# Causal attention values normalised on their way out of PSUM, by factors spread through DRAM

## The chip, the cores and the metric

One core of one Trainium2 chip runs the kernel; time is device microseconds of one execution, given as the median of several runs. The trace is of one profiled execution of the same program.

## The reference

Three stages over a batch of 4 with 448 tokens, in float32:

```python
# 1. twelve heads of 64: RMS-normalised q and k, softmax attention
q_n, k_n = rmsnorm(q, g_q), rmsnorm(k, g_k)
attn = softmax(q_n @ k_n^T / 8)            # denominators + 1e-9
x = heads_to_columns(attn @ v)             # [4, 448, 768]
# 2. mixer: tokens, then channels (768 -> 1536 -> 768)
u = x + transpose(relu(x^T @ w_tok1) @ w_tok2)
x = u + relu(u @ w_ch1) @ w_ch2
# 3. four experts, each one causal head of 64; every token keeps its best two
logits = x @ w_gate
for e in range(4):
    a = softmax(causal(x @ wq[e] @ (x @ wk[e])^T / 8))
    out += gate[:, e] * (a @ (x @ wv[e]) @ wo[e])
```

The gate of a token is the softmax over its best two logits, and 0 for the two other experts.

## The kernel before

All products are float32. The mixer and the projections split each operand into a high and a low part and run three passes on TensorE per product (`mm3`, line 625). Scores (line 707), attention values (line 830) and transposes (lines 731, 755 and 856) are float32 matmuls.

The batches go through the stages one after another. While batch b is in its channel mixer, the twelve heads of batch b + 1 run as six pairs in between (`pipeline`, `Pair`), and in front of them the two causal pairs of batch b - 1, whose expert projections (`project`) have just been made. Batch 2's causal pairs are scored between the channel mixer and the projections of batch 3, and batch 3's own come at the very end.

A pair's path is `score` (`weighted`: scores into PSUM, row maxima on VectorE, exponentials on ScalarE with row sums as a by-product; `flip` or `turn`: the weights transposed, so that keys lie on partitions) and `finish` (`attend`: the product with the values into a PSUM tile `av`, whose rows are 2 x 64 value columns and whose columns are the 448 queries). What remains is the division by the row sums, which lie on partitions, one per query, while `av` has queries along its columns. The kernel has two ways for that:

- The heads of batches 1 to 3 use `spread`: the inverse sums are turned into rows, written to DRAM, and read back broadcast over 64 partitions as a tile `rn`; `attend` then multiplies `av` by `rn` as it takes it out of PSUM (line 849). For pairs with queries in blocks of 112 (not `wide`) `spread` has a memset, an addition, a reciprocal, a 32-square transpose (`tni`), four DMA writes and two broadcast reads.
- The causal pairs, and the heads of batch 0, use `normalize`: `av` is copied to SBUF (`oT`), transposed by four matmuls per pair (line 856) so that queries lie on partitions, and multiplied by inverse sums (times the gate, for causal pairs) as it leaves PSUM into a tile `nat` (line 875). `combine` then transposes each half back by four matmuls, copies it out of PSUM and subtracts for the low part (line 1291), and multiplies with `wo` to make the output.

No instruction's place is left to a queue or to the compiler: every step is planned (`Plan.add` with an estimated cost, what it reads and writes, the engines that it may run on) and then issued in an order that stands in a constant, `TABLE`, with the engine of each step. The table was found by annealing, starting from a list scheduler (`lay`), which charges TensorE extra for a change of mode: `TURN` and `ENTRY`, for "rows" (scores), "columns" (values) and everything else. DMAs go through SyncE's queue, in order. VectorE and GpSimd share a port.

The tile `nat` has one buffer, which also holds the q and k rows of the next heads for their mean squares. PSUM tiles: `m` (values, transposes) has 2 buffers, `a` (products) 2, `s` (scores) 2.

Of the kernel before, what the change touches and what calls it, by code (L numbers as in the profile page):

```python
# [12 lines left out]
F32 = mybir.dt.float32  # L13
# [48 lines left out]
    r";`m5Bd2`j?+}<c+%~Mj&rCdmE3|=TH*f?d?$juYZ;$ZMdItlj+eAX-Qial?BK{3AURf|Y*>ZOM}A-l8{%R;G)W~)+=-KWrL4"
    r"LVI;@m=TZdM}GDoi%}lo=&eH|LBwU39=hih3C@7y&4U?SuurdO2q4Zohk2MOdIgYA<B@N_{JMT4B^6>0T+@f78jxKj@&^X?<"
    r"9A<zOdxg-hV;r`Q{f^A@ar5baHUeSc)MaBpjp;!nx=jP1}0sp_^XEp8`9ddwv`e>#%Zidgu$b=I;S6lk)e~T>kgdG4HjBt5#"
    r"3GZ%m)TudEw8`KIC<_MLeL6F@6kg1#^jD;LiR%w=Th0Q81<_1QdgWkzR$?c)h3x9?keKwYQKj)|-Kwc9LC(l^XQ3Ko_2-*y|"
    r"Yu>d`*Qn7hd(&x0#NGwdR%$W8%+dBNEkr`v2PsY0=P=RlxjNYHO5MO6<D`zh(&%k|cmjq(0IPYkAMk<TJMr9hvj$7>(U!*5h"
    r"=l^Xm27L_l-_OpWqyl}Ca1CBWpPfMaUHQ9Gg`l*`wwIp{{7~MJbvuBRqnB1Ep>^F^R2{mWN1z$oi$18s(Q>3$r1RBDStv`xw"
    r"%o(l@9I~^$ex}-mWW!Gj6FSYgx}ApO}dyAt;#6RIM1uTWBvJ*aP9Y*?Th=QmEtFUKiN(~@D#~v<dsy(-+Rz0;~+&@(wVG|XV"
    r"X{<ZU~PIxMM)+?q2P=M`am@Nwo71J=oXRBK1r)zfpqD2n8Lku%km0@!vuC<sj)?*D<Y<-`wA3L+-#BJNJLAr;OLG+)LTAlrc"
    r"Ex&@amh9UR>?1URw&>Is2wd7x?&1|T&FRROFYFH`m6%qLNB=F=J5t~t};Tq=q?xBTd})#>NUN_G!J2lg!R;8|&0PUVm9&Yuf"  # L70
    r"BhN`dszMHU*T8;nevtfY`o29P6j63J@SUt69XWtYy4G#nVNc!ijhug7xDO*~6L(t(>P&c@wMXLoT&>CC!ZC|+UU`ZZ3`uNfZ"
    r"$?A!#e&EuD288ZQS#+!;Cy);Ycm832tViLRZ9~7DyLA$;_@7C$O~W_;xH+%KW0RIIIfSH1m?`!oa;Ojfsu$|*5A&1mdFbN@E"
    r"}QQJYNj}kw0eNFpHp!vrNilLdOJAfy?)o)@R6igx9-@0R)diS%t5u-pIQ~cbfNy)KP6Nb4S%QNUXXeuG;+|AB07OS-F17;uL"
    r"&)G1tO?TxO>w?_H1Iah6zIkaS)OV$&<v^Kp(>1eHm|kyu9!Yhn8>cH}Sn|(64a-$Var{mff#oWYA%OGwZ}!8&LtaRd=oZg!I"
    r"LPd&=-qIriQDpBGVlJzhEhXB?;Je-|d;rH=;S<NbW;boR{jiPc!o7<Xm;6PXhWYZ0Qaj(hF#AirA&%p`@-uN6F4^D~?aXqfX"
    r"n!8y#plaC6{cmg@}lvr@z6U{MoIi?kelP_<58A-8a__Xido)3(9C%g&El5zE>>*rRa=U+E@`82}p0^~OP@Ro6}Va7e#e|Z6u"
    r"#;s{RbLUeXe|+S|6DwNG!1**ZPF;nD_dquWM+lkg$#Mk7B(ADhQaN=)3M7hOlH@WD!MrW7WA;NE`kgy~ql+IRNQfbW-Lxw7%"
    r"*t==HWmGVfsMs<4<}v3?DX)htAXpJUm|2*#hO(okVKM>=($$SXDy2S?T%EQlz?1Nft<)O<W%s(di>$ExY`g(3D28~$6ok30$"
    r"S1~!Xw2S9oCPS(eu)im;5|z`pXC}4v-y49){!2ANbv_0g;>J@{r0>P{=|8?q7-X;J5O7?zwJe5xARmbC=buxp&QN;JHE#e}_"
    r">uY**#OSQS}J5Ne1e=Dkgp?%26)PM=@P`|rkxf!Ul56Kdb-)wb67Q}F)$xouJQ_<bUY5#C~Jf_2%aA}erB=Wxd9Y<5p%`Kf#"  # L80
    r"GbjtmB3!?-)8Zi4xp59;EH{6CT>kGyvq&@K`A?x$KJVrO*?CRrKkr2A=IjP{aNIEHxvaGYUi8Xig^L6>lyZnrSJDt(ZQTM?x"
    r"irO``g`Y99ed($+##mnMGY_Fz6dzEhp(2|!e}CQ;KVdiDccnxof7gBu-pbBi?7yvl<dXr|%4mHKPI0#=V`mFX@5fD_Ef%9i9"
    r"X8&@-3uY|^A=}BazlO*KRfm-U$tk{k@kDq1TwR}2{-4bCnB+ap)(o}N!7bZ1FifhkERa%3%Yf#ywG3e^}BY532%6@XGe7e$@"
    r"#o&q{Pr)m!RMCq{D{Jhps(el3SBp6RG~1je3i8-`BG`v<(9)y5q;dIutZ?(Y5n3f8SjPa(FL4xNQ^Y?dxdE%(60Efjc?I))u"
    r"TAy8#%@Z>}Ya{)aBJ?pimN^ZEa-#%uy-!9kEtuv02*AZ0RP3+6n3;XuE+^sfiHRG<SrhDaq1T=(5Sj_p74Yuk3QH`hHelVX9"
    r"5oWtmtKbm(G;9_(BG5+7v@WM8JFaVS2zcJB{6(Emd%z`;9FolhK*=8g1wk+=WW2amD2O?8!(*EH_K^XW?|G<NTHNtHLGTvyH"
    r"Jj2;JfJtc20e;o3GLq4W=s;#p;E=a({*D}vA{-58I*gpCxovZpL$7uqej=y~ZXMRFZb;+tKE*xOrGAdf5Aq5M*NcCdgV*8!I"
    r"+9ap738TsY&Qg2X007s8&YvB%DROQGY4;ezh{fn$eR2F8utCMmb-TDLJxkuvO4LqbJEI|XVEA(1mt(H5eJ>4?Z`KG)NE_df!"
    r"QYX`ME!L2i6=%ATtToKSb8uk<9}w2o0y&@NGmg8~*i3_yA$yC9B^Z5Z*fEo>?s=<z<wI@nRP{kUJiWBVugf@=F-GoM7vq#Ku"
    r"rVh~sw4YqPsYI6W*MxrL)7vr?LsyqW&e9ymD|yA!fc<;rV25xNPHPXb47{JPusW$n;ga7gyLp4gQ^+40s-y&6OV7x2Ppv_AP"  # L90
    r"&kL)x2ZW~@JM@FHjaQ%pIy+lV)v2V2Y-d8Sha(4~?fSha*aVTz1K*Ig|=i^BG^onwNb>a_IY0k-k3RCqP3*^@Aq^~2KST|_v"
    r"Te#zj{Ud6>DZl<QzM$;QMmv^+)1zzm!l6NOE%x*hG=QUfw-n98ywI}l@8;t;w%i`OfrE(h(LO11Ce$2b?!DloaH_cSyEA7}q"
    r"pUhF#8WSnZmEyZIv!p=5B?Orio>@vJHXpo%S(7KNRI|<9Qx)gp@GNqF_PCT+U5J&z*X}Wi0SpwG<5sA8*U`RS-#>k=O`{OJc"
    r"Rn`4&`VbgS#Dki(uzNoqpt9=DCNKV%m#nk*w#+5?sd1;6{Ny&ZTxNDf1X|x8JyIvdxxXqlQIvQ_V5TKllAHxpm1E$Efq^fTQ"
    r"W?#2-{jME_N?Hja23!$U2~-yD^Q!vXx%W+$e=sWdH+s?P*0!6Rk7gaJ!jU>qcP0S_zwP2$ojgeE~)JckILpm1!KDI14K=dnv"
    r"UQgYzF!U$Kn0OS=$!!=Tq&2N-*yVEz^l6AI0%ra+ztV%Sz-Du|v9JH$B)fh^B+U7Kz$%n!uUR}Hu*UDy<eX1Tw3uo6Os}zCO"
    r"Cwbsoo#q<aoDe1as2IOqNjQQqw<j&(IN#HpYZeyE-ju=-^2=Y>A}Im+70s6N8SL&ihHS+UL8u>!RRxIfhoQpdd;)5@vW9oEk"
    r"-~DJJ7HJrw*TPpl9<Q#_a%)}9-_NDHSpB)avLj|zjoeZ^XG=^M_wt0MM`Fd!qXQb^oRoL>`-xcVaP0yLD#bcX9wv$OFW#=MX"
    r"1}+mq+%qkLX+9UQ>d)tA@WrhCelf&be<F_kS!-Jk~Xzl<pq6d4!Ek`Jvflu3f*f)C)F}E~=o{%Mhoki+OktdE{+kALS>L1O+"
    r"-M;+1`7vb}m5R@nAX*!+~p91-zX6%7Y%3M<fHSr+5}^q+h&eZ=&K_=dy87h~=U21nfzC;Ya$VPxp7d<}Eu8wLC;Tq~9`CigO"  # L100
# [1312 lines left out]
```

## Time and profile before

| | before |
|---|---|
| time of 3 runs | 839.68 us median, 838.71 to 841.11 |
| the profiled execution | 838.88 us, of which 837.1 us are the span of the trace |
| TensorE matmuls | 810.9 us busy, 97% of the span |
| VectorE, ScalarE, GpSimd | 614.6, 465.9 and 154.8 us |
| granted TensorE clock | 1.00 of full in every stretch but the last (0.97) |
| DMA | 168.37 MB |

An engine's busy time is the union of its instructions; a matmul's record lasts longer than its turn in the stream, since matmuls are pipelined, so the start of one to the start of the next is the better price of one.

### The profile page before, as it was taken

The numbers are of one execution on the slowest core, as the hardware profiler recorded it, in microseconds if no ns is written. First come the engines' busy times: TensorE is split into PE (matmuls) and PEld (weight loads), VectorE is DVE, ScalarE is ACT, GpSimd is POOL, SyncE is SP. The second block draws the span as 40 slices with busy tenths as digits, with TensorE's granted clock in tenths as the row PEclk, the third lists the DMA queues.
The fourth block names the chain that finished last, engine by engine and source line by source line (L and its number), as shares of the span: only waits on it lengthen the run. The fifth ranks groups of instructions, "written<-read, shape, count | busy, mean of one in ns | idle before, by whom it ended". The sixth has DMA issues, their size and how long they took to land.

```text
span 837.1 us, 13116 instructions
## 1 busy us (share of the span) xinstructions
PE 810.9 (97%) x4508; PEld 630.6 (75%) x4508; DVE 614.6 (73%) x1292; ACT 465.9 (56%) x1033; POOL 154.8 (18%) x181
## 2 busy tenths in 40 slices
PE   4899999999999999999999999999999999999998
PEld 1446697887676869877777877877876898999786
DVE  7999898889998785568889688756498773224473
ACT  6988976767887533644577446334576531000233
POOL 3043411122352244010230214000021010000000
PEclk9999999999999999999999999999999999999999
DMA  8747878988777748877566515785645416766444
GB/s 237 198 143 208 274 242 274 322 274 284 253 253 189 259 150 259 281 202 200 175 194 161 165 60 154 242 272 175 209 135 161 136 50 194 207 210 208 127 139 170
DMA packets 83201, 168.37 MB, mean 201 GB/s; under 512 B 17504, under 2 KB 39136, under 8 KB 83136
## 3 DMA queue, kind: packets, MB, share of 16 engines
q1 hardware_dynamic: 82992, 167.54, 65.7%
q8 instruction: 36, 0.59, 0.3%
q14 instruction: 29, 0.24, 0.1%
q10 hardware_dynamic: 144, 0.00, 0.0%
HBM read 136.66 MB, written 30.84 MB: 200 GB/s over the span
## 4 chain that ended last, share of the span: by engine, by line
PE 82%; DVE 12%; ACT 3%; issue 2%; DMA 1%; POOL 0%; SPq 0%; ACTq 0%; DVEq 0%
PE a L625 58%; PE s L707 9%; PE m L830 9%; PE m L856 2%; DVE nm L677 2%; DVE s L805 2%; PE s L755 2%; PE a L731 1%; DVE s L817 1%; ACT s L692 1%; PE s L731 1%; DVE wraw L575 1%; DVE wraw L577 1%; DMA h<-in_nat_dram 1%; DMA kept_c<-whl 0%
## 5 line engine op out<-in xcount | busy, mean ns | idle before, releaser
L625 PE MATMUL a<-uhl,whl 128*128 128x448 f32 x1152 | 242.9, 365 | 0.9 <-DVE hid L1203 0.9
L625 PEld LDWEIGHTS a<-uhl,whl 128*128 128x128 f32 x1152 | 213.3, 188 | 27.9 <-issue 8.7
L625 PE MATMUL a<-hid,whl 128*128 128x448 f32 x864 | 182.0, 365 | 0.8 <-DVE whl L555 0.7
L625 PEld LDWEIGHTS a<-hid,whl 128*128 128x128 f32 x864 | 160.0, 188 | 24.2 <-issue 6.4
L692 ACT ACTIVATE s<-s,nm,st 128x448 f32<-128x448 f32 (+1 forms) x192 | 137.3, 723 | 57.5 <-DVE nm L683 29.5
L817 ACT COPY s<-s 32x896 f32<-32x896 f32 (+1 forms) x118 | 102.5, 868 | 28.1 <-DVE s L805 18.4
L707 PE MATMUL s<-k,q 64*128 64x448 f32 (+4 forms) x512 | 110.1, 545 | 4.8 <-ACT s L692 3.9
L677 DVE TENSOR_REDUCE nm<-s 128x2 f32<-128x896 f32 (+1 forms) x96 | 101.6, 1080 | 13.0 <-PE s L707 12.5
L830 PE MATMUL m<-s,v 128*64 128x448 f32 x384 | 77.5, 545 | 0.9 <-POOL whl L555 0.9
L707 PEld LDWEIGHTS s<-k,q 64*112 64x112 f32 (+1 forms) x512 | 41.1, 183 | 44.6 <-issue 23.7
L1214 DVE TENSOR_TENSOR u<-a,u 128x448 f32<-128x448 f32 x48 | 29.8, 621 | 58.0 <-PE a L625 57.7
L805 DVE STREAM_TRANSPOSE s<-s 128x896 f32<-128x896 f32 x60 | 63.1, 1088 | 8.2 <-ACT s L692 4.3
L555 POOL TENSOR_TENSOR uhl<-u,uhl 128x448 fp32r<-128x448 f32 x31 | 35.9, 1172 | 175.7 <-DVE uhl L537 115.6
L692 ACT ACTIVATE s<-s,nm 112x336 f32<-112x336 f32 (+3 forms) x64 | 31.1, 492 | 63.0 <-DVE nm L671 61.7
L817 DVE COPY s<-s 32x896 f32<-32x896 f32 (+1 forms) x95 | 61.3, 645 | 2.3
L830 PEld LDWEIGHTS m<-s,v 128*64 128x64 f32 x384 | 25.6, 136 | 44.4 <-issue 40.9
L541 ACT ACTIVATE hid<-a 128x448 fp32r<-128x448 f32 x28 | 15.2, 544 | 76.2 <-PE a L625 76.2
L555 POOL TENSOR_TENSOR whl<-wraw,whl 128x384 fp32r<-128x384 f32 (+1 forms) x30 | 31.0, 1040 | 101.3 <-ACT whl L536 58.9
L1203 DVE SCALAR_TENSOR_TENSOR hid<-a,hid 128x448 fp32r<-128x448 f32 x48 | 29.9, 622 | 26.8 <-ACT hid L541 26.1
L625 PE MATMUL a<-whl,uhl 128*112 128x260 f32 x288 | 40.2, 289 | 0.1
L536 ACT ACTIVATE s<-s 112x448 f32<-112x448 f32 (+5 forms) x53 | 23.1, 484 | 30.2 <-PE s L755 24.8
L692 ACT ACTIVATION_READ_ACCUMULATOR s<-s,nm,st 128x1 f32 (+1 forms) x192 | 38.3, 199 | 0.0
(148 smaller groups left out, 1055.4 us busy)
## 6 DMA issues: line engine op xcount, KB each, us to landing
whl<-kept_c SPq DMA_DIRECT2D x144, 384.0 KB, 3.9
w<-in_wc_dram SPq DMA_DIRECT2D x48, 384.0 KB, 3.7
kept_c<-whl SPq DMA_DIRECT2D x48, 384.0 KB, 5.1
whl<-kept_qk SPq DMA_DIRECT2D x24, 384.0 KB, 3.0
nat<-in_nat_dram SPq DMA_DIRECT2D x19, 448.0 KB, 5.9
v<-in_vals_dram SPq DMA_DIRECT2D x24, 256.0 KB, 4.4
q<-in_qkt_dram SPq DMA_DIRECT2D x24, 232.0 KB, 3.9
k<-in_qkt_dram SPq DMA_DIRECT2D x22, 224.0 KB, 4.4
```

The source lines that it names most:

```text
L536: lambda e: nc.scalar.activation(dst(), src(), AF.Copy) if e == "ACT"
L555: either(n, reads, writes, lambda e: e.tensor_tensor(dst()[:, 1], src(), f(dst()[:, 0]), op=ALU.subtract))
L625: nc.tensor.matmul(acc, lhs[:, x], rhs[:, y], start=first and i == 0, stop=last and i == 2)
L677: lambda e: e.tensor_reduce(nm.t[:R, c], pst.t[:R, :, :w], axis=AX.X, op=ALU.max, negate=True))
L692: lambda j=j: nc.scalar.activation(s.t[:, c, j, :w], pst.t[:R, j, :w], AF.Exp, bias=nm.t[:R, c, j : j + 1], scale=-1.0 if rq is None else ...
L707: nc.tensor.matmul(pst.t[:R, j, :w], q.t[me, CP * c : CP * c + R], k.t[me, :w], start=True, stop=True)
L731: nc.tensor.transpose(ps()[:, i, CP * r : CP * r + CP], s.t[:, r].rearrange("p j k -> p (j k)")[:, P * m : P * m + P], ident[:CP, :CP])
L805: dve(2 * S - 4, [(s, (j, r)) for j in range(2)], [(t, r)], lambda e, r=r: e.transpose(t.t[:, :, 32 * r : 32 * r + 32], s.t[:, r].rearrang ...
L817: lambda e, a=a, o=o, w=w, at=at: (nc.scalar.copy if e == "ACT" else ENG[e].tensor_copy)(at(p.t[32 * o : 32 * o + 32, :, P * a : P * a + N ...
L830: nc.tensor.matmul(av.t[64 * j : 64 * j + 64, q0:S], vat(j, c)[1](), p.t[:, j, c, q0:] if causal else p.t[:, 3 * j + c], start=c == 0, sto ...
L1203: lambda e, hl=hl, pa=pa: e.scalar_tensor_tensor(hl.t[:, 1], pa.t[:, :S], 0.0, f(hl.t[:, 0]), op0=ALU.max, op1=ALU.subtract))
L1214: dve(S, [pa], [u], lambda e, u=u, pa=pa: e.tensor_add(u.t, pa.t[:, :S], u.t))
```

## The change

For the causal pairs of batches 0 to 2 the way of `normalize` is replaced by that of `spread`, with the inverse sums multiplied by the gate before they are spread. Their values leave PSUM already normalised, with columns along queries, which is the shape that `combine` multiplies with `wo`, so that only the split into high and low parts is left. Batch 3's causal pairs stay as they were. The planner has a third mode, "flips", for transposes, costs for each kind of change of mode, and slightly other costs for transposes; the table of the order is a new one for the whole program.

```diff
-    TURN = {None: 0, "rows": 220, "columns": 187}
-    ENTRY = 85
+    TURN = {
+        (None, "rows"): 90, (None, "columns"): 90, (None, "flips"): 3,
+        ("rows", None): 322, ("rows", "columns"): 215, ("rows", "flips"): 215,
+        ("columns", None): 294, ("columns", "rows"): 187, ("columns", "flips"): 187,
+        ("columns", "columns"): 190, ("flips", None): 85, ("flips", "flips"): 68,
+        ("flips", "rows"): 172, ("flips", "columns"): 120,
+    }
...
-                cost += (mode != now) * (self.TURN[now] if now else self.ENTRY)
+                cost += self.TURN.get((now, mode), 0)
...
         dve(80, [], [inv], lambda e: e.reciprocal(mine(), mine()))
+        if p.causal:
+            gt = ex[p.b][1]
+            dve(2 * NCH, [gt], [inv], lambda e: e.tensor_tensor(
+                mine().rearrange("p (j c) -> p j c", j=2),
+                mine().rearrange("p (j c) -> p j c", j=2),
+                gt.t[:, 0].rearrange("p c e -> p e c")[:, 2 * p.pr : 2 * p.pr + 2],
+                op=ALU.mult))
...
+            self.last = causal and b == B - 1
...
-        if p.causal or alone:
+        if alone or p.last:
...
-        if not p.causal and not alone:
+        if not alone and not p.last:
             spread(p)
...
         oT = attend(p.w, p.vat, p.causal, p.rn, p.wide)
+        if p.causal and not p.last:
+            two = quad.setdefault(p.b, [])
+            two.append(oT)
+            if len(two) == 2:
+                if later is not None:
+                    later.append((p.b, two))
+                else:
+                    combine(p.b, two)
+            return
...
             ohl.append((hl, o))
+            if b < B - 1:
+                split(S, o, lambda i=i: on[i].t, [on[i]], [hl])
+                continue
             pt = psm()
```

`split` casts the high part out of SBUF (ScalarE or VectorE) and subtracts it for the low part (VectorE or GpSimd).

## Rows read from the trace of the kernel before

**Rows 1.** The page's busy times: engine, us, share of the span, instructions.
```profile
PE 810.9 (97%) x4508; PEld 630.6 (75%) x4508; DVE 614.6 (73%) x1292; ACT 465.9 (56%) x1033; POOL 154.8 (18%) x181
```

**Rows 2.** The page's chain that ended last, shares by engine.
```profile
PE 82%; DVE 12%; ACT 3%; issue 2%; DMA 1%; POOL 0%; SPq 0%; ACTq 0%; DVEq 0%
```

**Rows 3.** Stretches: from:to, us, busy of each engine, clock, DMA share, GB/s.
```profile
0.00:20.00 20.00, 8.14 (x24) 3.30 (x24) 13.96 (x32) 12.92 (x23) 6.89 (x19) 1.00 0.83 232
...
300.00:320.00 20.00, 18.80 (x96) 14.55 (x95) 17.22 (x25) 11.03 (x26) 10.62 (x11) 1.00 0.51 167
...
500.00:520.00 20.00, 19.17 (x89) 14.50 (x88) 17.08 (x23) 11.70 (x22) 7.48 (x8) 1.00 0.44 134
```

**Rows 4.** TensorE's groups by shape: busy us, mean ns | idle before.
```profile
L856 PE MATMUL m<-ident,oT 128*112 128x128 f32 x128 | 18.1, 272 | 0.0
```

**Rows 5.** Timeline of TensorE, 290 to 310 us: start, us, what [idle before].
```profile
298.65 0.60 PE L856 MATMUL m<-ident,oT 128*112 128x128 f32 x4
299.01 1.31 PE L625 MATMUL a<-xhl,t 112*128 112x256 f32 x9
300.16 0.60 PE L856 MATMUL m<-ident,oT 128*112 128x128 f32 x4
300.69 1.77 PE L707 MATMUL s<-k,q 64*128 64x448 f32 x8
302.84 0.60 PE L856 MATMUL m<-ident,nat 112*128 112x112 f32 x4 [0.37 <-DVE nat L875]
303.79 0.60 PE L856 MATMUL m<-ident,nat 112*128 112x112 f32 x4 [0.34 <-DVE nat L875]
304.16 2.65 PE L625 MATMUL a<-t,h 128*128 128x448 f32 x12
307.26 1.44 PE L625 MATMUL a<-xhl,w 128*128 128x448 f32 x6 [0.45 <-DVE u L1185]
```

**Rows 6.** Timeline of TensorE, 487 to 506 us.
```profile
491.65 1.04 PE L856 MATMUL m<-ident,oT 128*112 128x128 f32 x8
492.61 1.77 PE L707 MATMUL s<-k,q 64*128 64x448 f32 x8
494.32 2.67 PE L625 MATMUL a<-xhl,t 112*128 112x256 f32 x21
496.83 0.93 PE L856 MATMUL m<-ident,nat 112*128 112x112 f32 x8
497.52 2.65 PE L625 MATMUL a<-t,h 128*128 128x448 f32 x12
```

**Rows 7.** Timeline of VectorE, 297 to 313 us.
```profile
299.90 0.98 DVE L1276 TENSOR_TENSOR gt<-gt,g 112x16 f32<-112x16 f32 x1
...
302.10 0.69 DVE L875 TENSOR_TENSOR nat<-m,rc 112x512 f32<-112x512 f32 x1
...
303.64 0.41 DVE L1167 SCALAR_TENSOR_TENSOR h<-a,h 128x256 fp32r<-128x256 f32 x1
...
306.50 1.15 DVE L1185 TENSOR_TENSOR u<-a,oT 128x448 f32<-128x448 f32 x2
...
308.10 0.38 DVE L537 CAST uhl<-u 128x448 fp32r<-128x448 f32 x1
```

**Rows 8.** VectorE's groups by shape.
```profile
L779 DVE RECIPROCAL inv<-inv 112x8 f32<-112x8 f32 x18 | 3.3, 189 | 0.2
```

**Rows 9.** Timeline of SyncE, 257 to 270 us: a trip of heads of batch 1.
```profile
260.24 0.33 SPq L781 DMA_DIRECT2D rn<-inv  x1
264.59 1.09 SPq L793 DMA_DIRECT2D rn<-rn  x2
```

**Rows 10.** DMA issues: count, KB each, median us from issue to landing.
```profile
rn<-rn SPq DMA_DIRECT2D x36, 112.0 KB, 3.4
```

**Rows 11.** What SyncE's queue waited for: us in total, times, longest.
```profile
SPq L616 <- PE a L625: 273.0, 145, 22.6
...
SPq L793 <- DMA rn<-inv: 22.7, 10, 5.5
```

More of the change, by code (lines that the diff above doesn't have):

```diff
@@ L62 @@
[L62 to L76, printed above, removed]
@@ L127 @@
[L127 to L130 removed]
+    r"c-n1Q33wDm+U~ci=gL9u1QJkgklU<s$>jkquE2v~Wj*-iRKyDuSQHc$Sp)@H<RQx?pm-p%D2S}$t_rK5BA^HeqJj{}MYuvjG"
@@ L131 @@
+    r"#1(xR<#X3k;`e7O3x|rfykhp_?Vj*5|gv2U=KZBn^{iIh*Fj3t{L0SWRvjJ0W(NZ;zjm<j2<N3zAQcT`r3-uIXphlJnGv5eX"
+    r"Sr*Wi!>_^%u27sH{_kbxV?lG?0@2_41f0o)^Ufz8+@zCL)y@HNVCWs3!|wQazVt3N14W`f`CpF1E~Us9<0df0#{!FwK?t*j_"
+    r";#$`cJc!vWrdfstfLHJ)&yo(9dpsd}yULCr-5+~Vyu3Xd>-3HBw>VAdw_)C0sy96`)z?t5nN&10&*5NA?7Dp=YEcxQa9te~M"
+    r"AMq;|P6{gU{bVy9?%11@{M9ahZ|5<Zd;Q"
 )
@@ L314, in lay @@
             if e == "PE":
-                if mode != now and now is not None:
+                if mode != now and now in ("rows", "columns"):
                     again = [x for x in avail[e] if steps[x[1]][5] == now and not taken[x[1]]]
@@ L741, in flip @@
                 heads = sorted({j for m in ms for j in (P * m // S, (P * m + P - 1) // S)})
-                add("PE", (110 if alone else 88) * NCH * n, [(s, (j, r)) for j in heads for r in range(NCH)],
-                    [pt], blocks(ms, at), 0.84)
+                add("PE", (96 if alone else 86) * NCH * n, [(s, (j, r)) for j in heads for r in range(NCH)],
+                    [pt], blocks(ms, at), 0.84, mode="flips")
                 copy(n * S, [pt], [(p, m) for m in ms],
@@ L757, in mms @@
                             s.t[:CP, r, j, CP * c : CP * c + CP], ident[:CP, :CP])
-            add("PE", 88 * (2 * NCH - 2 * cc - 1) - 10,
-                [(s, (j, r)) for r in range(cc, NCH)], [pst], mms, 0.84)
+            add("PE", 86 * (2 * NCH - 2 * cc - 1),
+                [(s, (j, r)) for r in range(cc, NCH)], [pst], mms, 0.84, mode="flips")
             for c in (cc, cc + 1):
@@ L772, in spread @@
         rn = sbuf([P, S], F32, "rn")
-        row = plan.buf(dr, [2, S], F32, f"rn_{p.b}_{p.pr}")
+        row = plan.buf(dr, [2, S], F32, f"rn_{p.b}_{p.pr}_{int(p.causal)}")
         if not p.wide:
@@ L856, in mms @@
                 nc.tensor.transpose(dst(c), src(c), ident[:p, :p])
-        add("PE", 4 * flip_ns(n), reads, writes, mms, 0.84)
+        add("PE", 4 * flip_ns(n), reads, writes, mms, 0.84, mode="flips")
     def normalize(oTs, sm, gate):
```

129 lines of the change are left out of this document (70 added, 59 removed).

## The prediction

> **What bounds the kernel now.** I read the busy times first. TensorE's matmuls cover 97% of the span, VectorE 73%, ScalarE 56%, GpSimd 18% [rows 1]; the span less TensorE's 810.9 us is 26.2 us. Busy time of pipelined matmuls proves little alone, so the chain that ended last comes next: 82% of it is TensorE, 12% VectorE, 1% DMA [rows 2]. The busy times by stretch say where TensorE is not the limit: the first 20 us hold 11.86 us of its idle time, and after them it is covered but for small holes, such as 1.20 us in 300:320 and 0.83 in 500:520 [rows 3]. VectorE is busy 17.2 and 17.1 of the 20 us there, so both engines are near their limit. What leaves TensorE's stream elsewhere should shorten the span; what leaves it near 300 and 500 does so only if VectorE keeps up.
>
> The timeline then shows what the causal heads' two turns cost. After batch 0 (298.65 to 307.26 us, [rows 5]): four transposes of the first value tile, nine passes, four more of the second, one score set, four transposes back, four more, and both times TensorE waits for VectorE's nat. After batch 1 (491.65 to 497.52, [rows 6]) the same work runs without a wait.
>
> **The change, part by part.** *The transposes that go.* In each of batches 0 to 2, two value tiles are turned by 4 transposes each and turned back by 4 each: 16 a batch, 48 in all. Their records last 272 ns [rows 4], but they overlap, so I price them by starts. A token-mixing pass of 256 columns takes (496.83 − 494.32)/21 = 0.12 us [rows 6]. From 298.65 to 300.16 is 1.51 us for four transposes and nine such passes [rows 5]; without the passes (1.08) that leaves 0.43, of which 0.36 lies up to the first pass (299.01) and 0.07 is that pass's delay of its successor. Eight in a row took 491.65 to 492.61, 0.96; some 0.1 of it is the entry into the score set, which comes in any case (the four from 300.16 took 0.53 with the same entry, against 0.43). So 0.86 for the first eight. The eight back took 0.69 (496.83 to 497.52), with 0.07 for the delay 0.76. Per batch 1.62, in three batches 4.9 us. The bounds are 4.2 (by the bare starts, 0.36 for four and 0.69 for eight) and 5.2 (all in separate fours of 0.43).
>
> The Trainium skill (TensorE: Matmul & The Clock Gate, Part 4: PE-mode transpose) puts one transpose in a kernel at about 275 ns, most of it access latency. The record's 272 ns agrees. Forty-eight at that figure would be 13.2 us, an estimate from the page; the starts say 4.9, since the next begins before the last has ended.
>
> *The waits that go with them.* At batch 0 the score set begins at 300.69; one lasts 1.71 (492.61 to 494.32, [rows 6]), so it ended at 302.40, and the transposes back start at 302.84: 0.44 lost. Between the two fours lie 0.95 us where 0.35 are needed: 0.60 more. I don't book the whole 1.04. The passes at 304.16 need h, which VectorE finished at 303.64 + 0.41 = 304.05, behind two nat multiplications of 0.69 in its queue [rows 5, 7]. With these gone h is there about 1.38 us earlier, at 302.7. So the passes move by 1.38, of which the transposes explain 0.76: 0.6 us net. Bounds 0 and 1.04.
>
> *VectorE and ScalarE.* Per batch go two copies of the values out of PSUM, two nat multiplications, three small operations on the sums and four evictions of the turned-back tile out of PSUM. In come two multiplications by the spread factors (nat's 0.69 for 512 columns, so 0.6 for 448), four small operations per pair (sum, reciprocal, gate, 32-square transpose; the reciprocal is 0.19 [rows 8], so 1.5 us a batch), a memset per pair on GpSimd, which is idle four fifths of the time, and two splits out of SBUF (a cast of 0.38 as for uhl [rows 7], and a subtraction that GpSimd may take). By count that is even on VectorE, a small gain on ScalarE, and I book nothing.
>
> *The queue and the trip.* Each of six pairs adds four writes and two reads: 36 issues on SyncE, 0.33 for a write and about 0.55 for a read [rows 9], 15 us in all. SyncE waits 273.0 us for TensorE to release weight buffers [rows 11], which hides the issues. An issue that waits for its row holds up the weight loads behind it, in before 2.3 us each in ten cases and 5.5 at most [rows 11]; six buffers of weights cover that in the dense stretches. Without the cover those 2.3 us would be lost up to six times, 14 us; nothing in before shows such a loss after the existing eighteen spreads.
>
> The trip's length is what matters. A write issued at 260.24 let the reads go at 264.59 [rows 9], 4.35 us; two issues 1.1; landing 3.4 [rows 10]; with the gate multiplication, the small transpose and three more writes (0.2 + 0.2 + 1.0) about 10 us from gate to factors. After batch 1 the old chain ran without a wait [rows 6], and batch 2's projections lie a whole channel mixer ahead of its causal pairs, so I see room there. After batch 0 the gate is ready only at 299.90 + 0.98 = 300.9 [rows 7], so the factors come at about 311, and after multiplication and split (0.6 + 0.38 + 0.6) the output products can begin at 312.5, where before has them at 307.26 [rows 5]. What they filled must be filled by something else: the two attentions, which need no factors, or the score set of 1.7 us. I take it that the new order does this, at no cost; the other end is in the first rival.
>
> *The order and the costs of changing mode.* The table replaces the whole order; the new costs of turning between scores, values and transposes act only through it. No row prices an order. The bounds I use: nothing gained, up to half of TensorE's idle time beyond the first 20 us, (26.2 − 11.9)/2 = 7 us gained, and as much lost. I take 0, as both signs are open.
>
> **The sum.** The profiled execution took 838.88 us, 837.1 in its span and 1.8 around it. 838.88 − 4.9 − 0.6 = 833.4. The median of the runs shown is 0.8 above that execution, the lowest 0.2 below; taken half-way I forecast **833.8**. A difference of 0.3% (2.5 us, so under 837.2 or over 842.2) is about what measuring this kernel can tell from no change.
>
> **Rivals.**
>
> *The removed work was filling holes.* The trip of batch 0 delays the output products by 5 us. VectorE adds u from 306.50 and casts it at 308.10 to 308.48 [rows 7]; with a subtraction as long as nat's multiplication behind it, it is there at 309.2. So the first channel products cannot fill 307.3 to 309.2: 1.9 us of TensorE idle. The same after batch 1 (VectorE 85% busy in 500:520) makes 3.8, and 833.8 + 3.8 = 837.6, no measurable change; with one of the two, 835.7. For it: both engines near their limit there [rows 3]. Against it: attentions and the score set can be moved in. The Trainium skill (DMA: Bandwidth & Descriptors, Anatomy of one DMA) gives a fixed cost near 2 us per DMA, mostly the write's receipt. Two of them, 4 us as an estimate, would bring the factors early enough that no such hole could open; the rows' 4.35 and 3.4 differ from it.
>
> *More than the sum.* The new order also closes holes that the old one left, a quarter of the 14.3 us outside the first 20: 3.6, so about 830. For it: the nat buffer no longer goes through the causal heads, so that natural loads come free earlier, and the planner now charges TensorE for transposes as the starts show. Against it: 12% of the chain is VectorE's [rows 2], and VectorE's work stays as long as it was. Should each transpose really occupy its recorded 272 ns, 13.1 us would go and the time be 825.8; the starts speak against that, and I give this 0.02 within this case.
>
> *VectorE stopped by the factors (slower).* VectorE takes its instructions in order. If the multiplication by the factors stands where nat's stands now, at 302, it waits until 311 and holds everything behind it: h, u, the row maxima. That is some 9 us of stop after batch 0, and I count the same after batch 1. TensorE can go on for about 2.7 us (the t, h products from 304.16), so 6 us are lost each time: 833.8 + 12 = 846. One such stop gives 839.8, no measurable change; slower needs over 8.4 us lost. Against it: in before, in the view of that line, no multiplication by spread factors waits for a DMA.
>
> *The new order is worse where the change has no business,* above all in the first 20 us, where TensorE has most of its idle time: a loss of 3 to 10 us, 837 to 844.
>
> **How the numbers follow.** Forecast 0.50, its own range 831.5 to 836.5; filling holes 0.16 (835.5 to 839); more than the sum 0.17 (826 to 831.5); VectorE stopped 0.08 (840 to 847); order worse 0.09. Faster takes the forecast, the third and a little of the others: 0.70. Same: most of the holes' case, half of the worse orders, one stop: 0.19. Slower: the rest, 0.11. The range cuts a tenth on each side: 829 to 840.
>
> **What would show it.** In the changed profile the transposes out of oT should fall from 128 to 104 and out of nat from 32 to 8, TensorE's busy time by about 5 us, with the same granted clock; rn reads should rise from 36 to 48. The stretch near 300 should show no wait for nat, and the output products of batch 0 about 5 us later with TensorE still busy. If VectorE there waits on rn, or TensorE's idle time beyond 20 us grows by more than 2.5 us, the rivals have it. What would make me wrong is an order whose holes differ by more than the 5.5 us that the step itself saves.

## The result and the profile after

The changed kernel takes **844.75 us** (median of 4 runs, 843.38 to 845.08), the kernel before 839.65 (838.71 to 841.11) beside it: ratio 1.0054 [1.0039, 1.0068]. It is 5.1 us slower; forecast were 833.8 us, range 829 to 840. The profiled execution took 844.99 us, 843.2 of them in its span.

The page of the changed kernel, its busy times and the chain by engine, beside [rows 1, 2] (PE is TensorE's matmuls, PEld its weight loads, DVE VectorE, ACT ScalarE, POOL GpSimd, SPq SyncE's queue):

```profile
PE 809.5 (96%) x4460; PEld 627.4 (74%) x4460; DVE 629.7 (75%) x1321; ACT 463.4 (55%) x1027; POOL 145.0 (17%) x181
...
PE 62%; DVE 12%; issue 3%; DMA 3%; ACT 2%; POOL 1%; SPq 0%; DVEq 0%; POOLq 0%; ACTq 0%
```

The 48 transposes are gone from the counts, but the span less TensorE's busy time is 33.7 us where it was 26.2, and VectorE is 15 us busier. The chain's 62% can't be set beside the 82% of before: followed back from its end, this chain stops at 130 us, so that its shares add up to 83%. Of the part that it covers TensorE has 74%; of the same part of before's chain it has 86%. The groups of transposes, by shape, and the DMA issues of the spread rows:

```profile
L869 PE MATMUL m<-ident,oT 128*112 128x128 f32 x104 | 15.3, 277 | 0.1
...
L869 PE MATMUL m<-ident,nat 112*128 112x112 f32 x8 | 1.1, 258 | 0.0
...
rn<-rn SPq DMA_DIRECT2D x48, 112.0 KB
```

128 became 104, 32 became 8, 36 became 48, as foretold: the change does what it says. The stretches, first those of [rows 3], then three that cover the first 800 us; columns as there (busy times of PE, PEld, DVE, ACT and POOL):

```profile
0.00:20.00 20.00, 6.59 (x20) 2.55 (x20) 12.09 (x26) 12.00 (x23) 7.51 (x20) 0.96 0.86 222
...
300.00:320.00 20.00, 19.29 (x127) 14.36 (x125) 18.77 (x41) 9.06 (x23) 4.66 (x5) 1.00 0.35 86
500.00:520.00 20.00, 19.86 (x113) 14.39 (x110) 12.89 (x20) 8.18 (x21) 3.20 (x5) 1.00 0.43 119
...
0.00:100.00 100.00, 82.53 (x460) 43.96 (x460) 87.61 (x180) 82.12 (x195) 27.76 (x48) 0.95 0.71 200
100.00:320.00 220.00, 208.86 (x1174) 161.85 (x1172) 206.81 (x433) 150.34 (x334) 61.87 (x69) 1.00 0.79 242
320.00:800.00 480.00, 478.55 (x2564) 388.35 (x2565) 313.25 (x629) 215.84 (x455) 54.20 (x63) 1.00 0.63 187
```

The same three long stretches of the kernel before:

```profile
0.00:100.00 100.00, 82.48 (x470) 44.14 (x472) 88.62 (x178) 86.37 (x208) 29.66 (x46) 1.00 0.75 210
100.00:320.00 220.00, 217.10 (x1229) 170.46 (x1226) 197.56 (x415) 153.24 (x345) 64.37 (x70) 1.00 0.78 249
320.00:800.00 480.00, 477.81 (x2593) 388.12 (x2591) 309.63 (x629) 213.17 (x444) 60.78 (x67) 1.00 0.60 180
```

Around 300 and 500 us, where the change has its business, TensorE is better covered than before. The loss lies from 100 to 320 us: its idle time there is 11.1 us against 2.9, and 8.2 of the 11.1 lie ahead of 262 us, before any step of the new way. VectorE is busy 206.8 us of these 220 against 197.6. The granted clock was below full in this profile's first 100 us (0.95), but TensorE's idle time is 17.5 us there in both kernels, and the two executions with a mean clock of 1.00 took 843.4 and 844.5 us.

One stall of that stretch, in the changed kernel's timelines of TensorE, VectorE and GpSimd (start, us, what):

```profile
237.47 1.48 PE L631 MATMUL a<-hid,whl 128*128 128x448 f32 x6
240.71 2.08 PE L631 MATMUL a<-uhl,whl 128*128 128x448 f32 x9 [1.75 <-DVE u L1237]
...
235.98 1.16 DVE L543 CAST uhl<-u 128x448 fp32r<-128x448 f32 x1
237.06 1.97 DVE L561 TENSOR_TENSOR uhl<-u,uhl 128x448 fp32r<-128x448 f32 x2
239.04 0.95 DVE L830 COPY s<-s 32x896 f32<-32x896 f32 x1
240.03 0.62 DVE L1237 TENSOR_TENSOR u<-a,u 128x448 f32<-128x448 f32 x1
...
235.89 1.00 POOL L561 TENSOR_TENSOR whl<-wraw,whl 128x384 fp32r<-128x384 f32 x1 [6.23 <-ACT whl L542]
237.42 1.13 POOL L561 TENSOR_TENSOR whl<-wraw,whl 128x384 fp32r<-128x384 f32 x1 [0.53 <-ACT whl L542]
238.61 0.84 POOL L830 COPY s<-s 32x448 f32<-32x448 f32 x1
```

TensorE stands 1.75 us until VectorE has added u. VectorE was never idle: its cast, begun 0.09 us behind a subtraction of GpSimd's, ended 0.25 us behind the subtraction's end, and took 1.16 us where such a cast took 0.38 in [rows 7]. The two subtractions and the copy behind it are long too, each beside GpSimd. The five instructions from 235.98 took 4.67 us; the experiments show the same five in 2.81.

**Lengthening.** I count it for every VectorE instruction as its duration less the tenth percentile of its own line and shape, where that is over 30 ns. Before: 27.5 us in all, 11.4 from 100 to 320 us; changed: 36.2 and 19.1. So 7.7 us more in the stretch where TensorE stands idle 8.2 us longer. There, 7.3 of the 11.4 us fall on 10 instructions that began beside a GpSimd instruction with two sources in the kernel before, and 16.0 of the 19.1 on 25 in the changed one. Over all of the changed kernel, and sorted by line: of 25 instructions that began on tiles in SBUF (L581, L583, L830, L561, L689) while a GpSimd instruction with two sources had over 0.2 us to go, every one was lengthened by the rest of that instruction less 0.10 to 0.14 us, and so were six of eight casts (L543); of 22 that take a tile out of PSUM (L683, L1190, L1237) the mean lengthening was 7 to 11 ns, and seven reciprocals and reductions with a single source in SBUF (L785, L946) were lengthened by 14 ns at most.

### The profile page after: what moved, and what is told of

It reads as the page before. It is cut to its first block, busy times and chain, and to the rows that moved or that the text cites. A ratio compares the mean times of both kernels' runs of the same rounds, so it can differ in the third digit from the quotient of the medians.

```text
span 843.2 us, 13072 instructions
## 1 busy us (share of the span) xinstructions
PE 809.5 (96%) x4460; PEld 627.4 (74%) x4460; DVE 629.7 (75%) x1321; ACT 463.4 (55%) x1027; POOL 145.0 (17%) x181
## 4 chain that ended last, share of the span: by engine, by line
PE 62%; DVE 12%; issue 3%; DMA 3%; ACT 2%; POOL 1%; SPq 0%; DVEq 0%; POOLq 0%; ACTq 0%
PE a L631 47%; PE s L713 6%; PE m L843 6%; DMA kept_c<-whl 2%; PE s L761 2%; DVE nm L683 1%; DVE wraw L581 1%; DVE s L830 1%; PE m L869 1%; DVE wraw L583 1%; DVE s L818 1%; DMA w<-in_wc_dram 1%; DVE whl L561 1%; POOL nat L951 1%; ACT s L698 1%
## 5 line engine op out<-in xcount | busy, mean ns | idle before, releaser
L631 PEld LDWEIGHTS a<-uhl,whl 128*128 128x128 f32 x1152 | 213.5, 188 | 32.6 <-issue 10.2
L830 ACT COPY s<-s 32x896 f32<-32x896 f32 (+1 forms) x120 | 100.6, 838 | 32.9 <-DVE s L818 27.9
L683 DVE TENSOR_REDUCE nm<-s 128x2 f32<-128x896 f32 (+1 forms) x96 | 101.9, 1081 | 11.1 <-PE s L713 10.8
L713 PEld LDWEIGHTS s<-k,q 64*112 64x112 f32 (+1 forms) x512 | 40.9, 183 | 49.7 <-issue 24.3
L1237 DVE TENSOR_TENSOR u<-a,u 128x448 f32<-128x448 f32 x48 | 29.8, 620 | 54.7 <-PE a L631 54.3
L830 DVE COPY s<-s 32x896 f32<-32x896 f32 (+1 forms) x101 | 67.9, 672 | 2.5
L561 POOL TENSOR_TENSOR uhl<-u,uhl 128x448 fp32r<-128x448 f32 x30 | 36.0, 1218 | 189.3 <-ACT uhl L542 101.3
L561 POOL TENSOR_TENSOR whl<-wraw,whl 128x384 fp32r<-128x384 f32 (+1 forms) x30 | 33.9, 1134 | 128.8 <-ACT whl L542 47.3
L698 ACT ACTIVATE s<-s,nm 112x112 f32<-112x112 f32 (+3 forms) x64 | 30.9, 492 | 37.1 <-DVE nm L677 34.9
L542 ACT ACTIVATE uhl<-u 128x448 fp32r<-128x448 f32 x26 | 14.9, 576 | 44.2 <-DVE u L1237 35.6
L631 PE MATMUL a<-whl,uhl 128*112 128x260 f32 x288 | 37.8, 286 | 0.8 <-DVE vg L543 0.7
L631 PEld LDWEIGHTS a<-whl,uhl 128*112 128x112 f32 x288 | 35.3, 175 | 4.4 <-issue 1.2
```

The source lines that it names most:

```text
L542: lambda e: nc.scalar.activation(dst(), src(), AF.Copy) if e == "ACT"
L561: either(n, reads, writes, lambda e: e.tensor_tensor(dst()[:, 1], src(), f(dst()[:, 0]), op=ALU.subtract))
L631: nc.tensor.matmul(acc, lhs[:, x], rhs[:, y], start=first and i == 0, stop=last and i == 2)
L683: lambda e: e.tensor_reduce(nm.t[:R, c], pst.t[:R, :, :w], axis=AX.X, op=ALU.max, negate=True))
L698: lambda j=j: nc.scalar.activation(s.t[:, c, j, :w], pst.t[:R, j, :w], AF.Exp, bias=nm.t[:R, c, j : j + 1], scale=-1.0 if rq is None else ...
L713: nc.tensor.matmul(pst.t[:R, j, :w], q.t[me, CP * c : CP * c + R], k.t[me, :w], start=True, stop=True)
```

## The experiments

Of the table's steps, 3,795 are the same in both kernels, 45 went, 84 came; about 400 of the same ones stand on another engine. All orders below were annealed or edited for these runs. The kernel before ran again beside each group of them, at medians of 839.32 to 840.94 us, so that times of different groups compare to 1 or 2 us. The table gives each run's median, its ratio to the kernel before beside it, TensorE's idle time and VectorE's lengthening from 100 to 320 us.

| kernel | us | ratio [95%] | idle | lengthening |
|---|---|---|---|---|
| before | 839.65 | 1 | 2.9 | 11.4 |
| changed | 844.75 | 1.0054 [1.0039, 1.0068] | 11.1 | 19.1 |
| old_order_old_way_replanned | 839.76 | 1.0001 [0.9985, 1.0018] | 3.0 | 11.0 |
| old_order_new_way | 836.08 | 0.9954 [0.9938, 0.9969] | 2.3 | 8.0 |
| old_order_to_262_then_new | 840.8 | 1.0013 [1.0003, 1.0024] | 5.3 | 16.7 |
| new_order_to_262_then_old | 846.27 | 1.0076 [1.0061, 1.0091] | 8.3 | 15.0 |
| old_order_more_vector_work | 842.68 | 1.0038 [1.0023, 1.0053] | 8.0 | 10.1 |
| new_order_less_vector_work | 842.35 | 1.0047 [1.0031, 1.0063] | 7.2 | 14.0 |
| new_order_four_raw_buffers | 843.9 | 1.0049 [1.0034, 1.0064] | 6.5 | 16.1 |
| new_order_both_edits | 844.08 | 1.0044 [1.003, 1.0058] | 6.5 | 14.2 |
| changed_less_vector_to_320 | 843.29 | 1.0039 [1.0024, 1.0054] | 8.3 | 16.8 |
| new_way_planned_with_margin | 837.0 | 0.9961 [0.9943, 0.9978] | 2.2 | 10.7 |
| new_order_gpsimd_zeros | 836.11 | 0.9951 [0.9936, 0.9966] | 3.4 | 5.9 |
| new_order_gpsimd_zeros_as_long | 835.26 | 0.9936 [0.9921, 0.995] | 3.4 | 4.4 |
| old_order_gpsimd_zeros | 833.18 | 0.9911 [0.9893, 0.9929] | 1.4 | 7.0 |
| changed_gpsimd_zeros | 830.77 | 0.9881 [0.9865, 0.9898] | 3.5 | 6.0 |
| before_gpsimd_zeros | 836.25 | 0.9954 [0.9939, 0.9969] | 1.0 | 6.5 |
| changed_subtract_in_thirds | 837.15 | 0.9957 [0.994, 0.9975] | 6.1 | 13.3 |
| old_order_subtract_in_thirds | 835.05 | 0.993 [0.9906, 0.9955] | 2.4 | 7.1 |
| margin_plan_subtract_in_thirds | 835.42 | 0.9938 [0.9922, 0.9955] | 2.6 | 12.4 |

**1. Is it the way or the order?** Four kernels with other tables: the way of the causal pairs and the place of every other step are taken apart.

```diff
-TABLE: new order, new way
+TABLE: old order and engines for the 3,795 steps, the new way's steps annealed in (old_order_new_way)
+TABLE: old order, old way, annealed in the same stretches (old_order_old_way_replanned)
+TABLE: old order to 262 us, the new one behind (old_order_to_262_then_new)
+TABLE: new order to 262 us, the old one behind (new_order_to_262_then_old)
```

> The causal pairs of batches 0 to 2 go the new way, but all steps outside three stretches (275 to 345, 465 to 535 and 765 to 845 us, where the causal pairs lie) keep the old order and the old engines; inside the stretches the steps are planned anew. Theory 'order' (the new way is worth the 5 us of transposes, and the new table loses some 10 us elsewhere): 833 to 836 us, TensorE's idle time in 100:260 near 2 us as in before. Theory 'way' (the trip through DRAM, the spread's VectorE work or the wait for the gate cost more than the transposes): 842 or more, with the idle time near 300 and 500.

> Control for the run before it: the kernel before, its own work unchanged, with the same three stretches planned anew by the same means. Theory 'order': 838 to 840, so that the run before it owes its gain to the new way and not to the planning. If planning anew alone gives 835 or less, the gain of the run before it says nothing of the new way. Theory 'way' has no say in this run: 838 to 840.

> The new way throughout. Steps that the old order has done by 262 us come in the old order on the old engines, all later ones in the order of the new table; 25 us behind the seam are planned anew to join them. No step of the new way lies before the seam. Theory 'order', with the loss before the seam (TensorE idle 8.2 us in 100:260 against 1.6 in before): 837 to 839. Theory 'way': 844 to 846, as the changed kernel, since all the new work is kept as it is there.

> The new way throughout. Steps that the new order has done by 262 us as in the new table, all later ones as in the first of these runs (old order, causal stretches planned anew). Theory 'order', with the loss before the seam: 840 to 843, that is the first run plus about 6.6. Theory 'way': the same as the first run within 1 us, at 842 or more.

It is the order. In the old one the new way gains 3.7 us, and annealing alone nothing. The new order up to 262 us, which holds no step of the change, costs 10.2 us; the part behind costs 4.7. Both are more than theory 'order' gave them (at most 843 and 839 us), and the two don't add up to the whole table's 8.7 us over old_order_new_way.

**2. VectorE's load or late weights?** The new table plans 5.9 us more VectorE work before 262 us, and VectorE is 95 to 99% busy from 200 to 260 us in the old order already; ScalarE also waits 17 us for raw weights between 100 and 262 us in new_order_to_262_then_old (16 in the changed kernel) where it waited 3.5 in the old order.

```diff
-copy (12 weight halves, 4 turned score tiles, 200 to 256 us): ACT
+copy: DVE                                  (old_order_more_vector_work)
-copy (15, 126 to 241 us): DVE
+copy: ACT                                  (new_order_less_vector_work)
-    "w3": 3    "oT": 8
+    "w3": 4    "oT": 7                      (new_order_four_raw_buffers)
```

> The old order with the new way (836.08 us), and one edit: 16 copies between 200 and 256 us (12 first halves of channel weights, 4 turned score tiles) go from ScalarE to VectorE in the table; the order of the steps stays. By the table's costs VectorE gets 5.8 us more there, ScalarE 8.6 us less. Theory V (the new table loses before 262 us because it gives VectorE 5.9 us more work there, and VectorE is 95 to 99% busy from 200 to 260 us): about +4 to +6 us, 840 to 842. Theory W (the loss is that the raw channel weights are read too late, because their three buffers come free too late): under 1.5 us, 836 to 837.5. Theory C (VectorE's load does not matter, only that its instructions stand in a bad sequence): under 2 us.

> The kernel with the new order to 262 us and the old one behind (846.27 us), and one edit: 15 copies between 126 and 241 us (10 first halves of channel weights, 3 flipped score tiles, 1 turned one, 1 first half of the channel's own product) go from VectorE to ScalarE in the table; the order of the steps stays. By the table's costs VectorE gets 6.2 us less, ScalarE 7.6 us more. Theory V: 4 to 6 us back, 840 to 842.5. Theory W: nothing back, 845.5 to 847. Theory C: under 2 us back, 844.5 to 846.5.

> The kernel with the new order to 262 us and the old one behind (846.27 us), and one edit: four buffers in place of three for the raw channel weights (room for it from seven in place of eight for the output tiles). Theory W: the reads start a buffer earlier, ScalarE's waits for them (17 us between 100 and 262 us) fall below 8 us, and 4 us or more come back, 842 or less. Theory V and theory C: 0, 845.5 to 847, even if ScalarE waits less.

Work added to VectorE there costs 6.6 us, so that stretch has no slack on VectorE. Taken away from the new order, 3.9 come back by the medians and 2.4 by the ratios (its runs scatter from 841.52 to 846.08): at the edge of what theory V said, or below it. The fourth buffer cut ScalarE's waits for raw weights from 17.2 to 3.7 us and 2.4 us came back, between the theories. Two more kernels, the two edits together, and the changed kernel with 36 copies moved and the buffer:

```diff
+copy (15): ACT, "w3": 4                    (new_order_both_edits)
+copy (36, 126 to 314 us): ACT, "w3": 4     (changed_less_vector_to_320)
```

> The kernel with the new order to 262 us and the old one behind (846.27 us), with both edits tried alone before: the 15 copies from VectorE to ScalarE (alone 3.9 us) and the fourth buffer for the raw channel weights (alone 2.4 us). If they are two causes, they add up: 839 to 841. If both only shorten one and the same wait for VectorE, the better of the two stands: 842 to 843.

> The changed kernel (844.75 us) with its whole order, the same 15 copies, 21 more between 247 and 314 us (weights, turned and flipped score tiles, token work) from VectorE to ScalarE, and the fourth raw buffer. By the table's costs VectorE gets 14.2 us less, ScalarE 17.6 us more. Theory V for both stretches (the new order loses before 262 us and again from 262 to 320 us since VectorE carries too much there): 6 to 9 us back, 836 to 839. Theory S (behind 262 us it is the sequence of the new steps that costs, not VectorE's load): 4 to 6 back from the first stretch alone, 839 to 841.

Both missed every theory. The edits together gain no more than either alone, and 14 us of VectorE work taken out of the changed kernel gain 1.5. Neither VectorE's load nor the weights can be the main cause. In these five kernels with the new order up to 262 us, unedited and edited, the lengthening stays at 14 to 17 us and the idle time at 6.5 to 8.3 (the changed kernel has 19.1 and 11.1).

**3. An order over the whole kernel,** with VectorE and GpSimd charged 6% more than their costs:

```diff
-TABLE: new order, new way
+TABLE: annealed anew; VectorE 535.8 us of planned work in place of 569.2, GpSimd 200.1 in place of 137.1
```

> The new way with an order annealed over the whole kernel, in which VectorE's and GpSimd's instructions were given 6% more than their cost; planned VectorE work 535.8 us in place of 569.2 in the changed kernel, GpSimd 200.1 in place of 137.1. Theory V: VectorE stops being the bound in 200 to 260 us, 826 to 832 us. If it is the slowing of VectorE by GpSimd on their shared port that cost the changed kernel its time, GpSimd's 63 us more would bring more of it: 836 us or above. Theory W: the raw weights are no earlier by design, 834 to 840.

837.0: no better than the old order, 5 us above what theory V gave, and where the other reading had it, that GpSimd slows VectorE. Theory W's range holds it too, so that this run does not decide between those two.

**4. Does GpSimd stop VectorE?** GpSimd's subtraction of the high part (the low half of a split value) reads two tiles in SBUF. Written as zeros it reads none; those low halves are left out.

```diff
-either(n, reads, writes, lambda e: e.tensor_tensor(
+either(n, reads, writes, lambda e: e.memset(f(dst()[:, 1]), 0.0)
+       if e is nc.gpsimd else e.tensor_tensor(
             dst()[:, 1], src(), f(dst()[:, 0]), op=ALU.subtract))
```

> The kernel with the new order to 262 us and the old one behind (846.27 us); in it GpSimd writes zeros into the low half of a split value where it subtracted before (those low halves are left out of the result; where VectorE makes them, it still subtracts). The subtractions are 37 of GpSimd's 46 us between 100 and 280 us. Theory P (what the new order lost is in good part that VectorE's instructions get longer while GpSimd works on the port that they share: 12.7 us of lengthening from 100 to 280 us, against 6.6 in the old order): the lengthening falls below 7 us and 4 to 7 us come back, 839.5 to 842.5. Theory L (only the number and cost of VectorE's instructions counts; the lengthening falls where VectorE has time): 845 to 847.

> The control to it: the old order with the new way (836.08 us), GpSimd writing the same zeros. Theory P: 1 to 3 us back, 833 to 835, so that the distance between the two orders shrinks from 10.2 us to 5 to 7. Theory L: 835.5 to 836.5, the distance stays at 10.

Theory P has the direction, and its sizes were too small: 10.2 us back in the new order (4 to 7 foretold), 2.9 in the old; the distance of 10.2 is down to 2.9 (5 to 7 foretold). But zeros are also quicker (0.43 us against 1.18 for weights) and wait for no input. So GpSimd was made as slow as before:

```diff
+c = (lambda x: x[..., :8]) if e is nc.gpsimd else (lambda x: x)
-e.tensor_tensor(dst()[:, 1], src(), f(dst()[:, 0]), op=ALU.subtract)
+e.tensor_tensor(c(dst()[:, 1]), c(src()), c(f(dst()[:, 0])), op=ALU.subtract)
+for _ in range(2 if e is nc.gpsimd else 0):
+    e.memset(f(dst()[:, 1]), 0.0)
```

> The kernel with the new order to 262 us and the old one behind (846.27 us); GpSimd subtracts only 8 columns of the low half, so that it waits for the same first half as before, and then writes zeros over the whole low half twice, so that it takes about as long as the whole subtraction did (2 x 0.42 us and some 0.15 us, against 1.10 us). Those low halves are left out of the result. In the trace VectorE's instructions on two tiles in SBUF are not lengthened beside the writing of zeros (0 to 8 ns over 18 cases) and are beside a subtraction (630 to 730 ns over 14). Theory P (the stop of VectorE behind a running subtraction): the gain of the zeros stays, 835 to 838.5. Theory G (GpSimd's low halves come late, and the zeros helped since they took 0.7 us less and did not wait): most of the gain goes, 842 to 846.

Its GpSimd groups for the weights, by shape, and the one of new_order_to_262_then_old that they replace:

```profile
L574 POOL MEMSET whl<- 128x384 f32 x54 | 22.8, 423 | 3.2
L572 POOL TENSOR_TENSOR whl<-wraw,whl 128x8 fp32r<-128x8 f32 x31 | 12.7, 408 | 123.7 <-ACT whl L551 73.9 <-DVE whl L552 31.6 <-DVE hid L1239 10.6
```

```profile
L570 POOL TENSOR_TENSOR whl<-wraw,whl 128x384 fp32r<-128x384 f32 x27 | 31.6, 1177 | 124.3 <-ACT whl L551 51.4 <-DVE whl L552 27.1 <-PE m L852 19.8
```

0.41 + 2 x 0.42 = 1.25 us against 1.18, behind the same inputs, and the time is 835.26. Theory G falls; it is VectorE that must not be stopped. The same for the two whole kernels:

> The changed kernel (844.75 us), whole, with GpSimd writing zeros once in place of its subtractions. Theory P for all of the new order: it comes within 3 us of the old order with the same zeros (833.18 us), 834 to 836.5. If behind 262 us another thing costs the 4.7 us that were measured there, 837 to 839.

> The kernel before (839.65 us) with the same zeros, the control to it. The old order lost 2.9 us to it with the new way (836.08 to 833.18): 836 to 837.5. With it the whole change is compared without GpSimd's subtractions: theory P says the changed kernel is then 0 to 3 us faster than this one, not 5 us slower.

830.77 against 836.25: the control came as foretold, the changed kernel 3 us below theory P's range. It is now 2.4 us faster than the old order with the same zeros (833.18), where it was 8.7 slower. **Without GpSimd's subtractions the change gains 5.5 us** (0.9881/0.9954 = 0.993, interval from the two [0.990, 0.995]); with them it loses 5.1. Zeros in place of the subtractions give the changed kernel 14.0 us back and the kernel before 3.4: the 10.6 between is what parts the 5.5 us gained from the 5.1 lost. The busy times of changed_gpsimd_zeros and of before_gpsimd_zeros:

```profile
PE 806.0 (97%) x4460; PEld 628.0 (76%) x4460; DVE 609.6 (73%) x1321; ACT 463.9 (56%) x1027; POOL 93.5 (11%) x181
```

```profile
PE 812.1 (97%) x4508; PEld 631.4 (76%) x4508; DVE 606.0 (72%) x1292; ACT 465.8 (56%) x1033; POOL 106.2 (13%) x181
```

And the stall shown above, in changed_gpsimd_zeros, TensorE and VectorE:

```profile
231.55 1.48 PE L632 MATMUL a<-hid,whl 128*128 128x448 f32 x6
232.87 1.98 PE L632 MATMUL a<-uhl,whl 128*128 128x448 f32 x9
...
229.88 0.39 DVE L543 CAST uhl<-u 128x448 fp32r<-128x448 f32 x1
230.19 1.16 DVE L562 TENSOR_TENSOR uhl<-u,uhl 128x448 fp32r<-128x448 f32 x2
231.36 0.68 DVE L831 COPY s<-s 32x896 f32<-32x896 f32 x1
232.07 0.62 DVE L1238 TENSOR_TENSOR u<-a,u 128x448 f32<-128x448 f32 x1
```

The same five instructions end 2.81 us after the first began (229.88 to 232.69), 1.86 less, and TensorE's wait of 1.75 is gone.

**5. A shorter stop, nothing left out.** If a stop lasts one GpSimd instruction, smaller instructions make shorter stops.

```diff
+k, w = (3 if e is nc.gpsimd else 1), dst().shape[-1]
+for i in range(k):
+    c = lambda x: x[..., w * i // k : w * (i + 1) // k]
-    e.tensor_tensor(dst()[:, 1], src(), f(dst()[:, 0]), op=ALU.subtract)
+    e.tensor_tensor(c(dst()[:, 1]), c(src()), c(f(dst()[:, 0])), op=ALU.subtract)
```

> The changed kernel (844.75 us), with nothing left out: each of GpSimd's subtractions is three instructions of a third of the columns. In the trace VectorE's instruction, once stopped, ends some 130 ns after GpSimd's running instruction would let it go, so that a stop can last only as long as one GpSimd instruction; a third takes an estimated 0.49 us (0.20 us for 4 columns, 1.10 us for 384) in place of 1.10 us, all three 1.5 us. Theory P with a stop that ends at the next instruction's boundary: VectorE's lengthening falls from 36 us to 15 to 24, and 3 to 8 us come back, 837 to 842. Theory R (the stop lasts as long as GpSimd has work queued): the three take longer than the one, 845 to 849.

> The old order with the new way (836.08 us), with the same subtraction in thirds, and nothing left out. Theory P with the stop ending at the boundary: 1 to 2.5 us back, 833.5 to 835. Theory R: 836.5 to 839.

> The new way in the order planned with margin (837.0 us; 35.5 us of VectorE's lengthening, GpSimd busy 203 us, and 826 to 832 us were expected), with GpSimd's subtractions in thirds and nothing left out. Theory P: this order missed its expectation for the same reason, since it gave GpSimd more to do; 3 to 6 us come back, 831 to 834. If it missed it because of the first 100 us and the end, where no order helps: 835.5 to 837.

The changed kernel gets 7.6 us back and beats the kernel before, although GpSimd is busier; its busy times, and its GpSimd group for the weights:

```profile
PE 805.9 (96%) x4460; PEld 626.2 (75%) x4460; DVE 621.0 (74%) x1321; ACT 463.4 (55%) x1027; POOL 174.7 (21%) x321
...
L566 POOL TENSOR_TENSOR whl<-wraw,whl 128x128 fp32r<-128x128 f32 x81 | 47.4, 614 | 109.6 <-ACT whl L542 45.9 <-DVE whl L543 24.0 <-PE m L848 19.5
```

174.7 us for GpSimd where it was 145.0. The lengthening fell from 36.2 us to 27.3 (15 to 24 were foretold), the idle time from 100 to 320 us from 11.1 to 6.1. Theory R falls. The old order gained 1.0 us, at the edge of theory P's range; at 835.05 it is the fastest kernel here that leaves nothing out, with the margin plan (835.42) beside it, whose gain of 1.6 lies within its runs' scatter and short of the 3 to 6 foretold. That the margin plan lost its gain to the stops is not shown: its lengthening from 100 to 320 us is no larger than that of the kernel before.

## Why the prediction was wrong

**The transposes that go, 4.9 us, and the waits that go with them, 0.6 us.** Right in kind, and too high in sum for the way alone. In the old order the new way gained 3.7 us (2.6 to 5.2 by its interval), and 3.1 with zeros on both sides (836.25 to 833.18). That the whole change gains just the 5.5 us of the sum where GpSimd writes zeros (836.25 to 830.77) is in part luck, since 2.4 of them come from the new order (833.18 to 830.77). TensorE's busy time was to fall by about 5 us at the same clock: it fell by 1.4 in the changed profile, whose clock in the first 100 us was 0.95 against 1.00, and by 6.1 between the two kernels with zeros. At 272 ns each the transposes would have been worth 13.1, which no gain here comes near; the price by starts stands.

**VectorE and ScalarE, nothing by count.** Right for the way itself: planned, 9.4 us of VectorE work goes and 9.2 comes. It missed that the table moves other steps between engines too, VectorE's plan going from 561.6 to 569.2 us.

**The queue and the trip, no cost.** Right. The changed kernel's TensorE around the output products of batch 0:

```profile
307.77 1.77 PE L713 MATMUL s<-k,q 64*128 64x448 f32 x8
309.48 2.68 PE L631 MATMUL a<-t,h 128*128 128x448 f32 x12
312.09 3.99 PE L843 MATMUL m<-s,vg 112*64 112x448 f32 x32
316.01 0.68 PE L631 MATMUL a<-xhl,w 128*128 128x448 f32 x2
317.40 1.07 PE L631 MATMUL a<-xhl,w 128*128 128x448 f32 x4 [0.71 <-DVE xhl L561]
```

The products start at 316.01, 8.75 later than in [rows 5] (5 were foretold; the whole stream is late by then), and the score set, mixer products and the attentions fill the room, as the step took for granted. No wait for nat is left, and in the stretches shown only 0.71 us for xhl. So neither the first rival (removed work was filling holes) nor a VectorE stopped by the factors came about. One aside of the first rival does not follow: with two DMAs at the 2 us that it takes from the Trainium skill, and its other terms (1.4 us of small work and writes, 1.1 for two issues, 1.6 for multiplication and split), the products could begin at 309.0, and a hole from 307.3 on would still have been open for 1.7 us. That section of the Trainium skill is also on DMAs that GpSimd issues, and these go through SyncE's queue.

**The order and the costs of changing mode: "I take 0, as both signs are open".** This step failed. The order costs 8.7 us (844.75 against 836.08, the new way in the old order), outside the bounds of 7 that I gave it, through stops of VectorE behind GpSimd's subtractions: with zeros in their place the same order is 2.4 us better than the old one. The rival of a worse order, at 0.09, was right in kind, and its 837 to 844 us all but held the result. Its place was wrong: I named the first 20 us, and it was 100 to 320. The test that I set (TensorE's idle time beyond the first 20 us up by more than 2.5 us) did answer: 14.3 before, 20.3 after.

What I could have read from the trace of before: VectorE's instructions there already carried 27.5 us of lengthening, 11.4 of it in the 220 us where VectorE was 90% busy. By what GpSimd's zeros gave it back, that cost 3.4 us of time. An order that puts 25 such pairs side by side in that stretch where there were 10, with VectorE on the way to TensorE, can cost many us, and my bound from TensorE's present idle time did not see it. The list scheduler does know the port (`lay` starts no step marked for it while the other engine's step holds it, `PORT`), but by planned times; the traces show that the pairs met all the same.

The Trainium skill (SBUF — State Buffer, SBUF: two separate sides) states the mechanism: VectorE and GpSimd share a pair of ports under an exclusive lock held for the whole instruction; with two inputs in SBUF, a VectorE instruction competes only against GpSimd instructions that read SBUF. The trace agrees: lengthening by the rest of GpSimd's instruction less 0.10 to 0.14 us, none over 20 ns for those of L683, L1190 and L1237 with a source in PSUM, and under 40 ns for two-source ones beside zeros. Casts and copies from SBUF to SBUF, which have one input, were lengthened too, and beside zeros as well (last section).

**What stays open.** Why the two halves of the new order (10.2 and 4.7 us) don't add up; how much of the loss goes by way of the late raw weights, for which one run gives 2.4 us and the run with both edits nothing on top (from 130 to 320 us the changed kernel's chain holds 24.7 us of DMAs where before's holds 3.7, but changed_gpsimd_zeros, the fastest of all, has 24.3 there too); and why thirds give back 7.6 of the 14.0 us that zeros give. The sum of lengthening does not order the kernels by itself: 13.3 us of it from 100 to 320 us go with 837.15, 14.2 with 844.08. That zeros help by not stopping VectorE, and not by being short, was run on new_order_to_262_then_old alone.

## What to carry to other kernels

An order of instructions is priced by what runs side by side, not by engine totals: before changing a table, list which instructions on a port that two engines share are on the way to the bounding engine, and how long each is held. Where one engine can stop another for a whole instruction, make the stopping instruction short, even if it then takes longer in sum. To tell a change from the plan that came with it, run the change in the old plan, and run both plans with the suspected cost taken out.

## What the hardware showed unexpectedly

- A subtraction of 384 columns on GpSimd (1.18 us) stopped a VectorE instruction on SBUF tiles for all that was left of it but some 0.13 us; three of 128 columns cost GpSimd 1.84 us (3 x 614 ns) and the kernel 7.6 us less.
- Writing zeros on GpSimd did not lengthen VectorE's two-source instructions (by under 40 ns in those of changed_gpsimd_zeros that began beside it), but it did lengthen casts and copies from SBUF to SBUF: all 20 that began beside it in the five kernels with zeros, with over 0.2 us of it to go, by 0.10 to 0.70 us, 0.27 on average.
- 14 us of work taken off VectorE, busy 94% of a stretch, gained 1.5 us, while making its stops shorter gained 7.6.
